# One PSUM bank per tile, weights loaded by ScalarE's queue among the tiles, in a retention and two-layer kernel

## The chip, the core and the metric

The kernel runs on one core of a Trainium2 chip. The metric is the device time of one launch in microseconds (us). Before the change three runs took 886.78, 886.79 and 888.87 us; their median is 886.79 us.

The core has five engines that run their own instruction streams and wait for one another by semaphores: TensorE (PE, matmuls into PSUM; its weight loads are listed as PEld), VectorE (DVE), ScalarE (ACT), GpSimd (POOL) and SyncE (SP). PSUM has 8 banks of 512 fp32 values in each of 128 partitions; a matmul writes into one bank. DMAs are issued from SP's or ScalarE's queue.

## The reference

```python
def _attn_ref(q, k, v):                  # q, k, v: 4 batches, 8 heads, 576 tokens, 64 per head
    scores = scale * np.matmul(q, k.transpose(0, 1, 3, 2))
    gamma = 1.0 - 2.0 ** (-5.0 - np.arange(H, dtype=np.float32))
    Dmat = np.where(rel >= 0, gamma[:, None, None] ** rel[None, :, :], 0.0)   # rel: row less column
    return np.matmul(scores * Dmat[None, :, :, :], v)

x = attn_out.transpose(0, 2, 1, 3).reshape(B * S, H * D)      # 2304 tokens x 512
h = x @ w_in;  r = np.maximum(h, 0.0);  x = (r * r) @ w_out   # first layer, 512 -> 2048 -> 512
h = x @ w_in2; g = h * np.clip(h + 3.0, 0.0, 6.0) / 6.0       # second layer
out = g @ w_out2
```

The weights arrive as 64-bit floats, two 32-bit words to a number. The kernel decodes them to fp32 on ScalarE and VectorE, and splits operands into a high and a low part for TensorE, so that a product of two fp32 matrices is three passes (high by high, high by low, low by high).

## The kernel before, in words

**Tiles.** Retention runs over 20 tiles of a batch's tokens (four full ones of 128 tokens and a last one of 64 for each batch, batches in pairs). In round `ti` of the loop TensorE makes the scores of tile `ti` (`stage_scores`), VectorE multiplies them by the decay (`ret`), and `values(ti - 1)` follows: scores by values (`stage_values`), the state's update (`stage_state`), queries by the state (`stage_queries`), VectorE's copy into `xall`, and ScalarE's copy of the state (`stage_state_copy`), which the queries of the next tile of the same batch, two rounds on, read. `values(ti)` ends by asking for the data of tile `ti + 5`, since there are five places for tiles (`TOKENS`). The first weights are loaded and decoded among the tiles.

**First layer.** The tokens are cut into four passes (`FIRST`: 768, 512, 512 and 512 tokens; called pass 0 to 3 here), each over 16 chunks of the hidden width. One unit is a pass and a chunk: `emit_h` (12 matmuls of 512 columns, 24 in pass 0), `emit_g` (ScalarE: relu, square, high part; VectorE: low part), a split of weights, and `y_steps` of the unit two back (`LAG`), four steps `m` of three matmuls. Chunk 15 is a pass's last: after each of its four steps ScalarE (even `m`) or VectorE (odd `m`) empties the finished bank into `xall`. In pass 0 the tokens above 512 have sums of their own, `ytail`.

**Second layer.** Three passes of 768 tokens (called A, B and C here), each over 8 pairs of chunks. A pair is seven products of six matmuls (`product`, into `hps`), and between the products run the 12 output steps of the pair before (`ywork`, three matmuls each, into six banks `yps`). In a pass's last six steps VectorE (even `m`) or ScalarE (odd `m`) empties each finished bank into a tile `o`, which a DMA stores.

**PSUM.** The eight banks are held as three tiles of two banks (`two_banks`, tags `p0` to `p2`) and two of one bank (`bank`, 6 and 7). Scores and values turn through the three pairs; the `yps` of steps 0 and 1 are two halves of one tile, those of 2 and 3 of the next, and `ytail` is the third. A wait is put between two instructions on two engines where they use the same tile.

**Order.** It is as written (`manual_schedule`); each engine runs its own instructions in that order. DMAs of both queues take turns in eight semaphores, called slots here: a DMA waits before its issue until the one that had its slot before has landed.

Of the kernel before, what the change touches and what calls it, by code (L numbers as in the profile page):

```python
# [9 lines left out]
F32 = mybir.dt.float32  # L10
# [4 lines left out]
ALU = mybir.AluOpType  # L15
# [9 lines left out]
C = 128  # L25
# [10 lines left out]
LAG = 2  # L36
# [31 lines left out]
def retention_moe_moe2(ctx, tc, qk, qk_last, kv, w_in, w_out, w_in2, w_out2, consts, out):  # L68
# [42 lines left out]
    def bank(i, shape, name):  # L111
        return banks.tile(shape, F32, tag=f"b{i}", name=name)

    ring = {"at": 0}

    def two_banks(i, shape, name):
        return banks.tile(shape, F32, tag=f"p{i}", name=name)

    def next_two(shape, name):
        ring["at"] += 1  # L120
        return two_banks(ring["at"] % 3, shape, name)


    staged = {}

    def load_w(l, c, which):
        turn["stage"] += 1
        if turn["stage"] <= 4:
            t = place(f"t{2 + turn['stage']}", [128, DM], mybir.dt.int64, "stage")
        else:  # L130
            t = stagep.tile([128, DM], mybir.dt.int64, tag="stage", name="stage")
        staged[l, c, which] = t
        if which == 0:
            t = t.rearrange("p (k f) -> p k f", k=KD)
            src = (w_in, w_in2)[l][:, c * 128:(c + 1) * 128].rearrange("(k p) f -> p k f", p=128)
            if l == 0:
                nc.sync.dma_start(out=t[:, ::2], in_=src[:, ::2])
                for e in range(2):
                    nc.sync.dma_start(out=t[64 * e:64 * e + 64, 1::2], in_=src[64 - 64 * e:128 - 64 * e, 1::2])
                return  # L140
        else:
            src = (w_out, w_out2)[l][c * 128:(c + 1) * 128, :]
        nc.sync.dma_start(out=t, in_=src)

    w32, first_in = {}, {}

# [51 lines left out]

    def make_decays():

        for e in range(2):
            nc.vector.tensor_tensor(
                out=decay[:, e], in0=mask.unsqueeze(1).to_broadcast([128, HP, C]),
                in1=gv[:, e].unsqueeze(2).to_broadcast([128, HP, C]), op=ALU.mult,
            )
        for e in range(2):
            own = slice(64 * e, 64 * e + 64)
            nc.vector.tensor_tensor(
                out=decay_last[own], in0=mask[own, own].unsqueeze(1).to_broadcast([64, HP, C // 2]),
                in1=gw[own].unsqueeze(2).to_broadcast([64, HP, C // 2]), op=ALU.mult,  # L210
            )
# [8 lines left out]
    def load_kv(ti):  # L220
        b, i, n = tiles[ti]
        kvt = place(TOKENS[ti % len(TOKENS)][1], [128, 2, H, D], F32, "kvt")
        if n == C:
            nc.sync.dma_start(out=kvt, in_=kv[b, C * i:C * i + n])
        else:
            for e in range(2):
                nc.sync.dma_start(out=kvt[64 * e:64 * e + 64, 1], in_=kv[b, C * i:C * i + n, 1])
        data[ti] += (kvt,)

    def load_tile(ti):  # L230
# [17 lines left out]
    def stage_scores(ti):  # L248
        b, i, n = tiles[ti]
        qkt = data[ti][0]  # L250
        r = place(("ret", "t2")[ti % 2], [128, 2, HP, C], F32, "ret")
        pe = next_two([128, 2, HP, C], "aps")
        for a in range(HP):
            for e in range(2):
                nc.tensor.matmul(  # L255
                    out=pe[keys(n, e), e, a, :n],
                    lhsT=qkt[64 * e:64 * e + 64, 0, a, :n],
                    rhs=qkt[64 * e:64 * e + 64, 1, a, :n],
                    start=True, stop=True,
                )  # L260
        if n == C:
            nc.vector.tensor_tensor(out=r, in0=pe, in1=decay, op=ALU.mult)
        for e in range(2 if n < C else 0):
            own = keys(n, e)
            nc.vector.tensor_tensor(
                out=r[own, e, :, :n], in0=pe[own, e, :, :n], in1=decay_last[own], op=ALU.mult
            )
        rets[ti] = r

# [26 lines left out]
    def stage_values(ti):  # L296
        b, i, n = tiles[ti]
        kvt = data[ti][1]
        r = rets.pop(ti)
        p = next_two([128, 2, 4, C], "vps")[:, :, :2]  # L300

        for a in range(HP):
            for e in range(2):
                to = e ^ a % 2
                nc.tensor.matmul(  # L305
                    out=p[64 * to:64 * to + 64, a % 2, a // 2, :n],
                    lhsT=kvt[keys(n, e), 1, 2 * a + e, :], rhs=r[keys(n, e), e, a, :n],
                    start=a < 2, stop=i == 0, skip_group_check=True,
                )
        return p  # L310

    def stage_queries(ti, p):
        b, i, n = tiles[ti]
        qkt = data.pop(ti)[0]
        for a in range(HP if i else 0):
            for e in range(2):
                own, to = slice(64 * e, 64 * e + 64), e ^ a % 2
                nc.tensor.matmul(
                    out=p[64 * to:64 * to + 64, a % 2, a // 2, :n],
                    lhsT=states[b % 2][i % 2][own, a, :], rhs=qkt[own, 1, a, :n],  # L320
                    start=False, stop=True, skip_group_check=True,
                )
        t = b * S + C * i
        by_bank = lambda x: x.rearrange("p (k j) t -> p j k t", j=2)
        nc.vector.tensor_tensor(
            out=by_bank(xall[:, :, t:t + n]), in0=p[:, :, :, :n], in1=by_bank(gq[:, :, :n]), op=ALU.mult
        )


    def parts(pos):  # L330
# [52 lines left out]
    def emit_h(pos, c):  # L383
        w = wins.pop((pos, c))
        hs = []
        for k, (o, n) in enumerate(parts(pos)):
            h = bank(6 + (c % 2 if pos else k), [128, 512], "hps")[:, :n]
            m = 0
            for kk in range(KD):
                for wp, xp in PASSES:  # L390
# [30 lines left out]
    def y_steps(pos, c):  # L421
# [2 lines left out]

        def step(m):
            if c == 0 and m == 0:
                yb[pos] = [t[:, b] for t in [two_banks(i, [128, 2, 512], "yps") for i in range(2)] for b in range(2)]
                if n > 512:
                    tail = two_banks(2, [128, 2, 2, 256], "ytail")
                    yb[pos] += [tail[:, b] for b in range(2)]  # L430
            w, y = wouts[pos, c], yb[pos]
            for k, (o, size) in enumerate(parts(pos)):
                p = y[m] if k == 0 else y[KD + m // 2][:, m % 2]
# [132 lines left out]
    def y_second(j, state):  # L566
# [3 lines left out]
        def work(w, gt, first, last):  # L570
            def step(m):
                if first and m == 0:
                    state["y"] = [
                        t[:, b] for t in [two_banks(i, [128, 2, DM], "yps") for i in range(n // 256)] for b in range(2)
                    ]
                p = state["y"][m]
                for e, (wp, gpart) in enumerate(PASSES):
                    nc.tensor.matmul(  # L578
# [113 lines left out]
    with tc.manual_schedule():  # L692
# [29 lines left out]
        for ti in range(len(tiles)):  # L722
# [2 lines left out]
                scale_keys(ti + 2)  # L725
            if ti:
                values(ti - 1)
            if 2 <= ti < 2 + AHEAD or ti >= len(tiles) - 4:
                load()
            if ti >= 8 and ti % 2 == 0 and halves[0][0] < -1:  # L730
                decoding = decode(*halves.pop(0)[1:])
                decoding.pop(0)()
                decoding.pop(0)()
            elif decoding:
                for f in decoding:
                    f()
                decoding = []
                next_load()
            if ti in (11, 13, 15, 17):
                split_x(0, (ti - 11) // 2)  # L740
            if ti in (14, 16):
                split_in(0, (ti - 14) // 2, nc.gpsimd)
        values(len(tiles) - 1)
        assert halves[0][0] == -1 and len(xs) == KD and not decoding

        units = [(pos, c) for pos in range(len(FIRST)) for c in range(NCH)]
# [153 lines left out]
```

## Time and profile before

| | |
|---|---|
| Runs | 886.78, 886.79, 888.87 us |
| The profiled execution | 885.24 us, of which the span from first to last instruction is 883.4 us |
| TensorE busy | 844.1 us, 96% of the span, in 4962 matmuls |
| VectorE, ScalarE, GpSimd busy | 524.3, 460.7 and 136.1 us |
| DMA | 184.22 MB, mean 209 GB/s |
| Retention, first layer, second layer | 0 to 70 us, 70 to 492 us, 475 to 883 us |
| Matmul of 512 columns, in the second layer's output steps | 396 ns mean of one; 0.23 us from start to start |

The profiled execution is one run, and its time stands 1.55 us below the median of the three. Matmuls are pipelined: one's duration overlaps the next one's, so that three take 0.70 us from the first's start to the start of what follows. Where idle time is named, it is the time the engine's instructions did not cover, and the name behind it is the one whose end released it.

### The profile page before, as it was taken

How to read it: one execution, taken by the hardware profiler on the slowest of the kernel's cores; microseconds unless marked ns; L12 is line 12 of the kernel's file. 1: busy time of each engine (PE TensorE's matmuls, PEld its weight loads, DVE VectorE, ACT ScalarE, POOL GpSimd, SP SyncE). 2: the span in 40 equal slices, each digit the busy share in tenths (PEclk: the TensorE clock that was granted, in tenths of full speed). 3: DMA queues.
4: the chain of work that ended last, by engine and by line, in shares of the span. 5: the costliest groups of instructions: out<-in, count | busy, mean ns of one | idle time of the engine just before them, and what ended most of it. 6: DMA issues, size and time to landing. Idle time of an engine off the chain costs nothing.

```text
span 883.4 us, 13348 instructions
## 1 busy us (share of the span) xinstructions
PE 844.1 (96%) x4962; PEld 726.7 (82%) x4962; DVE 524.3 (59%) x861; ACT 460.7 (52%) x878; POOL 136.1 (15%) x116
## 2 busy tenths in 40 slices
PE   8799999999999899989999899998999998999997
PEld 7688888887888688868888788897798887788885
DVE  5587777784777767775656445546345546344433
ACT  2257777785777667775665333345333345333332
POOL 2141323321433143312220000000000000000000
PEclk9999999999999999999999999999999999999999
DMA  9983656664777677785685454652664652664521
GB/s 364 322 303 100 194 173 187 190 213 147 256 276 276 226 253 264 272 294 181 224 308 193 164 206 155 215 179 94 257 220 155 214 180 88 261 223 155 210 76 72
DMA packets 67650, 184.22 MB, mean 209 GB/s; under 512 B 6656, under 2 KB 23168, under 8 KB 67584
## 3 DMA queue, kind: packets, MB, share of 16 engines
q1 hardware_dynamic: 66864, 182.22, 59.1%
q10 hardware_dynamic: 720, 1.15, 0.4%
q8 instruction: 39, 0.64, 0.3%
q14 instruction: 27, 0.22, 0.1%
HBM read 147.16 MB, written 36.18 MB: 208 GB/s over the span
## 4 chain that ended last, share of the span: by engine, by line
PE 86%; DMA 4%; ACT 4%; DVE 3%; issue 1%; POOL 0%; SPq 0%; ACTq 0%; DVEq 0%
PE yps L578 22%; PE hps L391 21%; PE hps L612 20%; PE yps L435 19%; PE ytail L435 2%; DMA qkt<-in_qk_dram 1%; DMA kvt<-in_kv_dram 1%; DMA stage<-in_w_in_dram 1%; PE vps L305 1%; DVE o L588 1%; PE aps L255 1%; ACT v L623 1%; ACT r L412 1%; ACT r L411 1%; DMA cst<-in_consts_dram 0%
## 5 line engine op out<-in xcount | busy, mean ns | idle before, releaser
L578 PE MATMUL yps<-wo,g 128*128 128x512 f32 x864 | 229.9, 396 | 12.3 <-DVE o L588 12.3
L435 PE MATMUL yps<-g,wo 128*128 128x512 f32 x768 | 198.3, 395 | 12.1 <-ACT xall L448 11.5
L578 PEld LDWEIGHTS yps<-wo,g 128*128 128x128 f32 x864 | 159.9, 189 | 39.4 <-DVE o L588 15.4
L435 PEld LDWEIGHTS yps<-g,wo 128*128 128x128 f32 x768 | 140.0, 189 | 42.7 <-ACT xall L448 14.8
L391 PE MATMUL hps<-xring,win 128*128 128x512 f32 (+1 forms) x720 | 154.7, 363 | 0.3 <-ACT r L411 0.3
L391 PEld LDWEIGHTS hps<-xring,win 128*128 128x128 f32 x720 | 124.1, 190 | 21.9 <-ACT r L411 0.5
L612 PE MATMUL hps<-xlast,win 128*128 128x384 f32 x576 | 117.9, 340 | 0.0
L612 PEld LDWEIGHTS hps<-xlast,win 128*128 128x128 f32 x576 | 104.7, 190 | 8.8
L417 DVE TENSOR_TENSOR g<-r,g 128x512 fp32r<-128x512 f32 x64 | 47.4, 740 | 76.1 <-ACT g L413 75.7
L631 DVE TENSOR_TENSOR u<-hps,u 128x384 f32<-128x384 f32 x48 | 26.8, 558 | 107.7 <-PE hps L612 107.7
L612 PE MATMUL hps<-xop,win 128*128 128x384 f32 x432 | 87.3, 336 | 0.0
L411 ACT ACTIVATE r<-hps 128x512 f32<-128x512 f32 x80 | 44.0, 550 | 82.5 <-PE hps L391 82.5
L612 PEld LDWEIGHTS hps<-xop,win 128*128 128x128 f32 x432 | 77.6, 188 | 6.6
L625 ACT ACTIVATE g<-c 128x384 fp32r<-128x384 f32 x72 | 37.8, 525 | 84.3 <-DVE c L624 84.3
L623 ACT ACTIVATE v<-c,three 128x384 f32<-128x384 f32 x72 | 44.4, 617 | 36.4 <-DVE c L631 35.4
L391 PE MATMUL hps<-xown,win 128*128 128x512 f32 x240 | 60.2, 392 | 0.0
L650 ACT ACTIVATE c<-hps 128x384 f32<-128x384 f32 x24 | 11.8, 492 | 80.3 <-PE hps L612 80.3
L167 DVE TENSOR_SCALAR a<-a 128x512 f32<-128x512 f32 x64 | 38.5, 602 | 24.7 <-ACT a L163 24.7
L391 PEld LDWEIGHTS hps<-xown,win 128*128 128x128 f32 x240 | 45.3, 190 | 9.3
L187 ACT ACTIVATE win<-w 128x512 fp32r<-128x512 f32 x64 | 39.7, 620 | 24.2 <-DVE w L182 24.1
L412 ACT ACTIVATE r<-r 128x512 f32<-128x512 f32 x80 | 47.2, 590 | 2.6
L624 DVE SCALAR_TENSOR_TENSOR c<-v,c 128x384 f32<-128x384 f32 x72 | 40.0, 555 | 13.4 <-ACT v L623 13.4
(76 smaller groups left out, 987.2 us busy)
## 6 DMA issues: line engine op xcount, KB each, us to landing
wo<-kept SPq DMA_DIRECT2D x96, 512.0 KB, 5.0
win<-kept SPq DMA_DIRECT2D x72, 512.0 KB, 3.6
kept<-ready SPq DMA_DIRECT2D x40, 512.0 KB, 3.8
stage<-in_w_out_dram SPq DMA_DIRECT2D x32, 512.0 KB, 4.3
qkt<-in_qk_dram SPq DMA_DIRECT2D x16, 512.0 KB, 8.3
kvt<-in_kv_dram SPq DMA_DIRECT2D x16, 512.0 KB, 8.7
kept<-wo SPq DMA_DIRECT2D x16, 512.0 KB, 5.1
stage<-in_w_in_dram SPq DMA_DIRECT2D x16, 512.0 KB, 4.1
```

What stands on the lines that cost most here:

```text
L167: nc.vector.tensor_scalar(out=a, in0=a, scalar1=LEAST, scalar2=MOST, op0=ALU.max, op1=ALU.min)
L187: nc.scalar.activation(out=hi, in_=src, func=ACTF.Copy)
L391: nc.tensor.matmul(out=h, lhsT=w[:, wp, kk * 128:kk * 128 + 128], rhs=xs[pos, kk][xp][:, o:o + n], start=m == 0, stop=m == 3 * KD - 1,)
L411: nc.scalar.activation(out=r, in_=hs[k], func=ACTF.Relu)
L412: nc.scalar.activation(out=r, in_=r, func=ACTF.Square)
L417: nc.vector.tensor_tensor(out=lo, in0=src, in1=hi.bitcast(F32), op=ALU.subtract)
L435: nc.tensor.matmul(out=p, lhsT=w[:, wp, m * 128:m * 128 + 128], rhs=g[pos, c][k][:, gpart, :size], start=c == 0 and e == 0 and not (k and ...
L578: nc.tensor.matmul(out=p, lhsT=gt[m // 3][:, gpart, m % 3 * 128:][:, :128], rhs=w[:, wp], start=first and e == 0, stop=last and e == 2,)
L612: nc.tensor.matmul(out=to, lhsT=wl[k][:, half, wp, o], rhs=x[:, xp, f], start=first and m == 0, stop=last and m == 5, skip_group_check=True,)
L623: nc.scalar.activation(out=v, in_=c, func=ACTF.Relu, bias=three)
L624: nc.vector.scalar_tensor_tensor(out=c, in0=v, scalar=6.0, in1=c, op0=ALU.min, op1=ALU.mult)
L625: nc.scalar.activation(out=hi, in_=c, func=ACTF.Copy)
```

## The change

1. **PSUM.** Every PSUM tile is one bank. `two_banks` is gone; `next_bank` turns through banks 0 to 5 for scores and values (two tiles each), later through banks 4 to 7 for `hps` from the third unit of pass 1 on. `yps` are banks 0 to 3 (0 to 5 in the second layer), the two tiles of `ytail` banks 4 and 5. VectorE's product of scores and decay, and its copy of the values, become two instructions, one for each bank.
2. **Weights among the tiles.** The first seven loads are issued from ScalarE's queue and not from SP's, at rounds 1, 3 and 5 (before: 2, 3 and 4) and in the last four. Decoding begins at round 6 and not 8.
3. **Last tiles.** The 64 tokens' values are loaded to both halves of the partitions by one DMA and not two.
4. **Decays.** GpSimd makes half of `decay`, and `decay_last` is made after round 1.

```diff
--- before.py
+++ after.py
@@ -111,20 +111,18 @@
     def bank(i, shape, name):
         return banks.tile(shape, F32, tag=f"b{i}", name=name)
 
-    ring = {"at": 0}
-
-    def two_banks(i, shape, name):
-        return banks.tile(shape, F32, tag=f"p{i}", name=name)
-
-    def next_two(shape, name):
+    ring = {"at": 0, "from": 0, "n": 6}
+
+    def next_bank(shape, name):
         ring["at"] += 1
-        return two_banks(ring["at"] % 3, shape, name)
+        return bank(ring["from"] + ring["at"] % ring["n"], shape, name)
 
 
     staged = {}
 
     def load_w(l, c, which):
         turn["stage"] += 1
+        queue = nc.scalar if turn["stage"] <= 7 else nc.sync
         if turn["stage"] <= 4:
             t = place(f"t{2 + turn['stage']}", [128, DM], mybir.dt.int64, "stage")
         else:
@@ -134,13 +132,13 @@
             t = t.rearrange("p (k f) -> p k f", k=KD)
             src = (w_in, w_in2)[l][:, c * 128:(c + 1) * 128].rearrange("(k p) f -> p k f", p=128)
             if l == 0:
-                nc.sync.dma_start(out=t[:, ::2], in_=src[:, ::2])
+                queue.dma_start(out=t[:, ::2], in_=src[:, ::2])
                 for e in range(2):
-                    nc.sync.dma_start(out=t[64 * e:64 * e + 64, 1::2], in_=src[64 - 64 * e:128 - 64 * e, 1::2])
+                    queue.dma_start(out=t[64 * e:64 * e + 64, 1::2], in_=src[64 - 64 * e:128 - 64 * e, 1::2])
                 return
         else:
             src = (w_out, w_out2)[l][c * 128:(c + 1) * 128, :]
-        nc.sync.dma_start(out=t, in_=src)
+        queue.dma_start(out=t, in_=src)
 
     w32, first_in = {}, {}
 
@@ -198,11 +196,13 @@
 
     def make_decays():
 
-        for e in range(2):
-            nc.vector.tensor_tensor(
+        for e, engine in enumerate((nc.vector, nc.gpsimd)):
+            engine.tensor_tensor(
                 out=decay[:, e], in0=mask.unsqueeze(1).to_broadcast([128, HP, C]),
                 in1=gv[:, e].unsqueeze(2).to_broadcast([128, HP, C]), op=ALU.mult,
             )
+
+    def make_last_decay():
         for e in range(2):
             own = slice(64 * e, 64 * e + 64)
             nc.vector.tensor_tensor(
@@ -223,8 +223,8 @@
         if n == C:
             nc.sync.dma_start(out=kvt, in_=kv[b, C * i:C * i + n])
         else:
-            for e in range(2):
-                nc.sync.dma_start(out=kvt[64 * e:64 * e + 64, 1], in_=kv[b, C * i:C * i + n, 1])
+            twice = kv[b, C * i:C * i + n, 1].unsqueeze(0).to_broadcast([2, n, H, D])
+            nc.sync.dma_start(out=kvt[:, 1], in_=twice)
         data[ti] += (kvt,)
 
     def load_tile(ti):
@@ -249,21 +249,19 @@
         b, i, n = tiles[ti]
         qkt = data[ti][0]
         r = place(("ret", "t2")[ti % 2], [128, 2, HP, C], F32, "ret")
-        pe = next_two([128, 2, HP, C], "aps")
+        pe = [next_bank([128, HP, C], "aps") for e in range(2)]
         for a in range(HP):
             for e in range(2):
                 nc.tensor.matmul(
-                    out=pe[keys(n, e), e, a, :n],
+                    out=pe[e][keys(n, e), a, :n],
                     lhsT=qkt[64 * e:64 * e + 64, 0, a, :n],
                     rhs=qkt[64 * e:64 * e + 64, 1, a, :n],
                     start=True, stop=True,
                 )
-        if n == C:
-            nc.vector.tensor_tensor(out=r, in0=pe, in1=decay, op=ALU.mult)
-        for e in range(2 if n < C else 0):
+        for e in range(2):
             own = keys(n, e)
             nc.vector.tensor_tensor(
-                out=r[own, e, :, :n], in0=pe[own, e, :, :n], in1=decay_last[own], op=ALU.mult
+                out=r[own, e, :, :n], in0=pe[e][own, :, :n], in1=decay[:, e] if n == C else decay_last[own], op=ALU.mult
             )
         rets[ti] = r
 
@@ -297,13 +295,13 @@
         b, i, n = tiles[ti]
         kvt = data[ti][1]
         r = rets.pop(ti)
-        p = next_two([128, 2, 4, C], "vps")[:, :, :2]
+        p = [next_bank([128, 4, C], "vps") for j in range(2)]
 
         for a in range(HP):
             for e in range(2):
                 to = e ^ a % 2
                 nc.tensor.matmul(
-                    out=p[64 * to:64 * to + 64, a % 2, a // 2, :n],
+                    out=p[a % 2][64 * to:64 * to + 64, a // 2, :n],
                     lhsT=kvt[keys(n, e), 1, 2 * a + e, :], rhs=r[keys(n, e), e, a, :n],
                     start=a < 2, stop=i == 0, skip_group_check=True,
                 )
@@ -316,15 +314,15 @@
             for e in range(2):
                 own, to = slice(64 * e, 64 * e + 64), e ^ a % 2
                 nc.tensor.matmul(
-                    out=p[64 * to:64 * to + 64, a % 2, a // 2, :n],
+                    out=p[a % 2][64 * to:64 * to + 64, a // 2, :n],
                     lhsT=states[b % 2][i % 2][own, a, :], rhs=qkt[own, 1, a, :n],
                     start=False, stop=True, skip_group_check=True,
                 )
         t = b * S + C * i
-        by_bank = lambda x: x.rearrange("p (k j) t -> p j k t", j=2)
-        nc.vector.tensor_tensor(
-            out=by_bank(xall[:, :, t:t + n]), in0=p[:, :, :, :n], in1=by_bank(gq[:, :, :n]), op=ALU.mult
-        )
+        for j in range(2):
+            nc.vector.tensor_tensor(
+                out=xall[:, j::2, t:t + n], in0=p[j][:, :2, :n], in1=gq[:, j::2, :n], op=ALU.mult
+            )
 
 
     def parts(pos):
@@ -384,7 +382,8 @@
         w = wins.pop((pos, c))
         hs = []
         for k, (o, n) in enumerate(parts(pos)):
-            h = bank(6 + (c % 2 if pos else k), [128, 512], "hps")[:, :n]
+            own = pos == 0 or pos == 1 and c < LAG
+            h = (bank(6 + (c % 2 if pos else k), [128, 512], "hps") if own else next_bank([128, 512], "hps"))[:, :n]
             m = 0
             for kk in range(KD):
                 for wp, xp in PASSES:
@@ -424,10 +423,9 @@
 
         def step(m):
             if c == 0 and m == 0:
-                yb[pos] = [t[:, b] for t in [two_banks(i, [128, 2, 512], "yps") for i in range(2)] for b in range(2)]
+                yb[pos] = [bank(b, [128, 512], "yps") for b in range(KD)]
                 if n > 512:
-                    tail = two_banks(2, [128, 2, 2, 256], "ytail")
-                    yb[pos] += [tail[:, b] for b in range(2)]
+                    yb[pos] += [bank(KD + b, [128, 2, 256], "ytail") for b in range(2)]
             w, y = wouts[pos, c], yb[pos]
             for k, (o, size) in enumerate(parts(pos)):
                 p = y[m] if k == 0 else y[KD + m // 2][:, m % 2]
@@ -570,9 +568,7 @@
         def work(w, gt, first, last):
             def step(m):
                 if first and m == 0:
-                    state["y"] = [
-                        t[:, b] for t in [two_banks(i, [128, 2, DM], "yps") for i in range(n // 256)] for b in range(2)
-                    ]
+                    state["y"] = [bank(b, [128, DM], "yps") for b in range(n // 128)]
                 p = state["y"][m]
                 for e, (wp, gpart) in enumerate(PASSES):
                     nc.tensor.matmul(
@@ -725,9 +721,9 @@
                 scale_keys(ti + 2)
             if ti:
                 values(ti - 1)
-            if 2 <= ti < 2 + AHEAD or ti >= len(tiles) - 4:
+            if ti in (1, 3, 5) or ti >= len(tiles) - 4:
                 load()
-            if ti >= 8 and ti % 2 == 0 and halves[0][0] < -1:
+            if ti >= 6 and ti % 2 == 0 and halves[0][0] < -1:
                 decoding = decode(*halves.pop(0)[1:])
                 decoding.pop(0)()
                 decoding.pop(0)()
@@ -736,11 +732,14 @@
                     f()
                 decoding = []
                 next_load()
+            if ti == 1:
+                make_last_decay()
             if ti in (11, 13, 15, 17):
                 split_x(0, (ti - 11) // 2)
             if ti in (14, 16):
                 split_in(0, (ti - 14) // 2, nc.gpsimd)
         values(len(tiles) - 1)
+        ring.update({"from": 4, "n": 4})
         assert halves[0][0] == -1 and len(xs) == KD and not decoding
 
         units = [(pos, c) for pos in range(len(FIRST)) for c in range(NCH)]
```

On TensorE, the end of pass 0 in the first layer (chunk 15's steps 1 to 3, then the `hps` of the next unit), before. `yps_1209` holds steps 0 and 1, `yps_1210` steps 2 and 3, `ytail_1211` all four tails:

```order
L435 MATMUL yps_1209<-g_2368,wo_2451 128x512 [waits Activation_49]
L435 MATMUL yps_1209<-g_2368,wo_2451 128x512 x2
L435 MATMUL ytail_1211<-gtail_1071,wo_2451 128x256 x3
L435 MATMUL yps_1210<-g_2368,wo_2451 128x512 x3
L435 MATMUL ytail_1211<-gtail_1071,wo_2451 128x256 [waits Activation_49]
L435 MATMUL ytail_1211<-gtail_1071,wo_2451 128x256 x2
L435 MATMUL yps_1210<-g_2368,wo_2451 128x512 [waits Activation_49]
L435 MATMUL yps_1210<-g_2368,wo_2451 128x512 x2
L435 MATMUL ytail_1211<-gtail_1071,wo_2451 128x256 x3
L391 MATMUL hps_2549<-xown_2212,win_2448 128x512 x2
```

The same place now; the four steps have tiles `yps_1281` to `yps_1284`, the tails `ytail_1285` and `ytail_1286`:

```order
L433 MATMUL yps_1282<-g_2443,wo_2526 128x512 x3
L433 MATMUL ytail_1285<-gtail_1143,wo_2526 128x256 x3
L433 MATMUL yps_1283<-g_2443,wo_2526 128x512 x3
L433 MATMUL ytail_1286<-gtail_1143,wo_2526 128x256 x3
L433 MATMUL yps_1284<-g_2443,wo_2526 128x512 x3
L433 MATMUL ytail_1286<-gtail_1143,wo_2526 128x256 x3
L390 MATMUL hps_2624<-xown_2287,win_2523 128x512 [waits Activation_49]
L390 MATMUL hps_2624<-xown_2287,win_2523 128x512
```

The three waits for ScalarE (`Activation`) inside the steps are gone, and the next unit's first matmul into `hps` waits for ScalarE, which it did not before: its bank, 5, is the one that held `ytail_1286`.

On TensorE, the last steps of pass A of the second layer (steps 0 to 5, between the products P5, P4 and P3 and the next pair's P1), before:

```order
L578 MATMUL yps_5029<-wo_5925,g_5782 128x512 x2
L578 MATMUL yps_5029<-wo_5925,g_5782 128x512 [waits DVE_49]
L578 MATMUL yps_5029<-wo_5925,g_5782 128x512 x2
L612 MATMUL hps_5986<-xlast_4880,win_5803 128x384 [waits DMAHW5_49]
L612 MATMUL hps_5986<-xlast_4880,win_5803 128x384 x5
L578 MATMUL yps_5030<-wo_5925,g_5782 128x512 x3
L578 MATMUL yps_5030<-wo_5925,g_5783 128x512 [waits DVE_49]
L578 MATMUL yps_5030<-wo_5925,g_5783 128x512 x2
```

and now:

```order
L574 MATMUL yps_5110<-wo_6009,g_5866 128x512 x2
L574 MATMUL yps_5111<-wo_6009,g_5866 128x512 x3
L608 MATMUL hps_6070<-xlast_4961,win_5887 128x384 [waits DMAHW1_49,DVE_49]
L608 MATMUL hps_6070<-xlast_4961,win_5887 128x384 x5
L574 MATMUL yps_5112<-wo_6009,g_5866 128x512 x3
L574 MATMUL yps_5113<-wo_6009,g_5867 128x512 x3
```

The odd steps wait for VectorE no more; the same holds for step 5 and for the other two passes' ends.

On ScalarE, the first rounds of tiles, before (`sps_172` and `sps_211` are the states of the two batches; each row with `x3` ends a tile's copy):

```order
L291 ACT_TABLE_LOAD [waits DMAHW0_49]
L291 ACTIVATE state_84<-sps_172,cst_81 128x64 [waits PE_49]
L291 ACTIVATE state_84<-sps_172,cst_81 128x64 x3
L291 ACTIVATE state_84<-sps_211,cst_81 128x64 [waits PE_49]
L291 ACTIVATE state_84<-sps_211,cst_81 128x64 x3
```

and now (`sps_175` and `sps_224`):

```order
L289 ACT_TABLE_LOAD [waits DMAHW0_49]
L289 ACTIVATE state_84<-sps_175,cst_81 128x64 [waits PE_49]
L289 ACTIVATE state_84<-sps_175,cst_81 128x64 x3
L135 DMA stage_194<-in_w_in_dram 128x2x128 [waits DMAHW2_49]
L137 DMA stage_194<-in_w_in_dram 64x2x128 [waits DMAHW4_49]
L137 DMA stage_194<-in_w_in_dram 64x2x128 [waits DMAHW5_49]
L289 ACTIVATE state_84<-sps_224,cst_81 128x64 [waits PE_49]
L289 ACTIVATE state_84<-sps_224,cst_81 128x64 x3
```

The three DMAs of a `w_in` load, with their waits for DMA slots (`DMAHW`), now stand in ScalarE's stream between one tile's state copy and the next one's.

## Rows read from the trace of the kernel before

**Rows 1.** waits of TensorE, whole span: engine, line, releaser, us in total, times, longest

```profile
PE yps L578 <- DVE o L588: 12.3, 9, 1.9
PE yps L435 <- ACT xall L448: 11.5, 7, 2.3
```

**Rows 2.** timeline of TensorE, end of pass 1: start, us, instruction, idle before

```profile
299.47 0.84 PE L435 MATMUL yps<-g,wo 128*128 128x512 f32 x3
302.64 1.66 PE L435 MATMUL yps<-g,wo 128*128 128x512 f32 x6 [2.33 <-ACT xall L448]
...
305.79 2.90 PE L391 MATMUL hps<-xring,win 128*128 128x512 f32 x12
```

**Rows 3.** chain of waits, end of pass 2: start us, us, what

```profile
387.57 2.73 PE hps L391 x12
...
402.13 2.74 PE yps L435 x12
```

**Rows 4.** windows, after those waits: us, five engines' busy, granted clock, DMA share, GB/s

```profile
396.00:398.00 2.00, 1.96 (x5) 1.57 (x6) 0.21 (x1) 1.10 (x2) 0.00 (x0) 0.50 0.02 6
```

**Rows 5.** timeline, end of pass 0, TensorE and ScalarE

```profile
205.35 2.90 PE L391 MATMUL hps<-xown,win 128*128 128x512 f32 x12
...
210.64 0.58 ACT L448 ACTIVATE xall<-yps 128x512 f32<-128x512 f32 x1
...
215.13 2.90 PE L391 MATMUL hps<-xown,win 128*128 128x512 f32 x12
```

**Rows 6.** timeline of TensorE, end of pass 3, beside the second layer's first products

```profile
482.48 1.22 PE L612 MATMUL hps<-xlast,win 128*128 128x384 f32 x6
483.54 0.86 PE L435 MATMUL yps<-g,wo 128*128 128x512 f32 x3
484.24 1.23 PE L612 MATMUL hps<-xlast,win 128*128 128x384 f32 x6
...
492.51 1.23 PE L612 MATMUL hps<-xop,win 128*128 128x384 f32 x6
```

**Rows 7.** chain of waits, second layer, the fifth product (P5) of five pairs

```profile
595.18 1.06 PE hps L612 x6
...
633.91 1.06 PE hps L612 x6
...
712.34 1.06 PE hps L612 x6
...
728.03 1.06 PE hps L612 x6
...
766.57 1.06 PE hps L612 x6
```

**Rows 8.** timeline, end of pass C, VectorE's first and ScalarE's last store tile

```profile
872.82 0.69 DVE L588 TENSOR_SCALAR o<-yps 128x512 f32<-128x512 f32 x1 [3.15 <-PE yps L578]
...
879.52 0.60 ACT L590 ACTIVATE o<-yps 128x512 f32<-128x512 f32 x1 [1.85 <-PE yps L578]
```

**Rows 9.** DMA issues, whole span: output stores, KB each, median us to landing

```profile
out_dram<-o SPq DMA_DIRECT2D x15, 256.0 KB, 2.0
```

**Rows 10.** windows among the tiles (columns as rows 4)

```profile
10.00:20.00 10.00, 8.78 (x172) 8.03 (x176) 5.16 (x6) 3.04 (x14) 3.57 (x4) 1.00 1.03 409
30.00:40.00 10.00, 5.86 (x153) 5.13 (x149) 5.55 (x12) 4.08 (x12) 0.73 (x1) 0.97 1.03 312
```

**Rows 11.** groups by line, whole span: VectorE's scores by decay; busy, mean ns, idle

```profile
L262 DVE TENSOR_TENSOR ret<-aps,decay 128x1024 f32<-128x1024 f32 x16 | 19.4, 1220 | 6.9 <-PE aps L255 6.9
```

**Rows 12.** timeline among the tiles: SP's issue of weights, VectorE's copies of values

```profile
14.46 3.07 SPq L139 DMA_DIRECT2D stage<-in_w_in_dram  x2
...
20.36 0.69 DVE L325 TENSOR_TENSOR xall<-vps,cst 128x512 f32<-128x512 f32 x1 [0.89 <-PE vps L318]
...
23.54 0.69 DVE L325 TENSOR_TENSOR xall<-vps,cst 128x512 f32<-128x512 f32 x1 [0.88 <-PE vps L318]
...
61.57 1.31 SPq L139 DMA_DIRECT2D stage<-in_w_in_dram  x2
```

## Prediction

> **What bounds the kernel now.** I read the waits of TensorE first, then the timeline and the chain of waits at the places they name, then the windows of the tile stage. TensorE is nearly always busy, so the question is where it is not. Two waits stand out [rows 1]: 12.3 us of the second layer's output steps on VectorE's store tiles, and 11.5 us of the first layer's on ScalarE's copies into `xall`. They fall only at the ends of passes. There a step is held until its neighbour, in the other bank of the same tile, has been emptied: the end of pass 1 shows step 1 starting 2.33 us late, behind ScalarE's copy of step 0, which lies in another bank [rows 2]. The idle time is not all of the loss: after the waits at the end of pass 2 the granted clock falls to 0.50, the 1.2 GHz level, while TensorE works on [rows 4]. I therefore price each place by its start-to-start time against an undisturbed stretch, which holds both.
>
> **The change part by part.**
>
> *Ends of passes in the first layer.* Twelve matmuls of 512 columns take 2.73 us undisturbed (the first row of rows 3, a unit's `hps`; its output steps have as many).
> - Pass 1: from the last unit's first output step to the next `hps` 305.79 - 299.47 = 6.32 us; less 2.73 that is 3.59 lost [rows 2].
> - Pass 2: from one `hps` to the output steps two blocks further on 402.13 - 387.57 = 14.56; less 3 x 2.73 that is 6.37 lost, the slow clock's share included [rows 3].
> - Pass 0: from `hps` to `hps` 215.13 - 205.35 = 9.78 [rows 5]. An undisturbed unit there is 12 matmuls of `hps` (2.73) and 12 + 12 of outputs, the second 12 with 256 columns (about half of 2.73): some 6.9. Lost: 2.9.
> - Pass 3: from product to product 492.51 - 484.24 = 8.27. Between them lie two products and three steps; a product takes 483.54 - 482.48 = 1.06, a step 484.24 - 483.54 = 0.70, so 4.22 was due and 4.05 are lost [rows 6].
>
> With a tile to each bank the order now shows no wait inside these steps. What is late next? In pass 1 the next pass writes its first step into bank 0 after one more `hps`; TensorE would be there 2.73 us after step 3, and ScalarE's copy of step 0, late as it is, ended by 302.64 [rows 2], against 299.47 + 2.73 + 2.73 = 304.93. So nothing of it comes back. At pass 0 something does. The third unit's `hps` goes to bank 5, which held the last tails, and waits for ScalarE's copy of them. ScalarE starts on the step-0 copy at 210.64, and four copies at 0.58 to 0.6 us with the last not before TensorE ends at 205.35 + 6.9 = 212.3 puts the release at about 213.1; TensorE waits 0.9 us of the 2.9 it was given [rows 5]. Gain of the four places: 2.0 + 3.6 + 6.4 + 4.05 = 16.0 us. Bounds: nothing of it from the 0.9 upward (17), or a copy's length (0.6) kept at each of the other three (14.2).
>
> *Ends of passes in the second layer.* The fifth product comes every 728.03 - 712.34 = 15.69 us. Two pairs across the end of pass A take 633.91 - 595.18 = 38.73, across that of pass B 766.57 - 728.03 = 38.54 [rows 7]: 7.35 and 7.16 lost. The steps' waits for VectorE are gone from the order. Late next is the store: there are three store tiles, so the fourth to sixth step's emptying needs the first three's DMAs landed, 2.0 us each [rows 9]. Steps now come about every 1.2 us (six steps and two products in 6.3). Putting VectorE's and ScalarE's instructions in their order, I estimate that the last emptying ends some 3 us after the last step; the weights for the next pair's second half stand behind that store in SP's queue, and would then be issued some 6 us before they are needed. I take the full 14.5; the lower bound, weights 2 us later than I reckon and both pass ends losing 1.5 us to it, is 11.5.
>
> *The end.* VectorE empties step 0 from 872.82 and ScalarE step 5 from 879.52 [rows 8]: 6.7 us for five steps that need 5 x 0.70 = 3.5 [rows 6]. The last store starts 3.2 us sooner. Six stores then come within 3.5 us instead of 6.7, and may cost one another something; I take 2.9, bounds 2 to 3.2.
>
> *Among the tiles.* Here the DMA engines bound the first half: their share is 1.03 from 10 to 20 us and from 30 to 40 [rows 10], and in the second of these TensorE is busy for only 5.86 of 10 us. The same bytes must land before the tenth tile, on whichever queue, so the weights' place in the queues (a round earlier, and beside SP's stream and not in it) moves which tile waits, not the sum; the decays and the first tile's VectorE work hide behind the same loads. The rate falls from 409 to 312 GB/s between the two stretches, with the same share. The Trainium skill ("DMA: Bandwidth & Descriptors", Issuing engines are not separate DMA queues) says that DMAs from several engines run on the same 16 DMA engines, and that a second issuing engine saves only the time to issue. By that the stage gains nothing but SP's time; were the low rate one queue's doing, 10 us at 312 would take 7.6 at 409 and the stage would gain about 2.4 us for each such stretch. The full share speaks for the rule, and I count nothing.
>
> VectorE pays for the smaller tiles. An instruction on 1024 elements takes 1220 ns [rows 11], one on 512 takes 690 [rows 12]: a fixed part of about 0.16 us, paid twice more in each of 20 rounds, 6.4 us of VectorE's time. Its cover is that a tile's product is needed only a round later (rounds are 23.54 - 20.36 = 3.18 us [rows 12], VectorE's share of them now 2.2), and the third decoding moves two rounds forward out of the stretch where it competed. If that cover fails in the last ten rounds, it costs 3 us; if the moved decoding relieves them, it returns 1.5.
>
> ScalarE pays for the issues. Two of the three DMAs of a `w_in` load held SP for 3.07 us among the early tiles, waiting for slots, and for 1.31 in the last rounds [rows 12]. On ScalarE they stand before the next state copy, which TensorE needs two rounds, 6.4 us, later; so nothing is due early. In the last four rounds ten issues at about 0.65 (half of 1.31), some 6 us, delay the first decoding after the loop by about that, less the idle time that ScalarE had there, and the first layer's first units by 0 to 1.5 us; I take 0.5. The single load of the last tiles' values saves SP an issue of 0.6 us in each of four rounds, and up to 1 us of transfers; I take 1 for it. Sum of the stage: -0.5 us, bounds -4 to +4.
>
> *Sum.* 16.0 + 14.5 + 2.9 + 0.5 = 33.9 us from the profiled execution's 885.24 (a span of 883.4 and 1.84 around it): 851.3. The median of the runs is 1.55 above the profiled one, so I add that: 852.9, rounded to 853.
>
> **The rivals.**
> *ScalarE becomes the bound at the passes' ends.* It does what it did, in the same order, and TensorE arrives sooner: if at each of the six places the next pass's first write meets a bank not yet empty, the wait comes back there, up to the 2.33 us that it was [rows 2], or 2 us at each, 12 in all: 865. For it: ScalarE's copy of step 0 ended 3 us after step 0 began. Against it: there are a whole `hps` block or a product and a step in between.
> *The clock stays low.* The granted 0.50 [rows 4] might belong to the stretch and not to the waits. Pass 2 lost 6.37 where pass 1, with the same order, lost 3.59, so 2.8 us are the clock's; as much again at the ends of passes A and B makes 8.4 not returned, 861. Against it: a stretch with more idle time spread over it, 10 to 20 us, has 1.00, the 2.4 GHz level [rows 10].
> *ScalarE is held by DMA slots* (slower). The place is the rounds with a load. If the slot of a load's DMA is still in flight, ScalarE stands, and behind it the state copies, then TensorE's queries. A hold of H costs H - 6.4 us beyond the two rounds of slack; it eats the 33.4 us gained elsewhere if each of seven loads holds ScalarE for more than 11.2 us, three to four times the 3.07 seen on SP [rows 12]. At 12 us each the time would be 885.24 + 1.55 - 33.4 + 7 x 5.6 = 893.
> *The tiles of one bank don't remove the waits*, because they are the banks' own: 887. The order has no such wait left, and the waited-for step lies in another bank.
>
> **How the numbers follow.** A measurement here can tell a change of about 0.3%, 2.7 us, from none. My forecast (853; its own range 848 to 860) gets 0.78, ScalarE at the passes' ends 0.09, the clock 0.05, a tile stage that gains more than I allow 0.03, ScalarE held 0.03, no effect 0.02. Low end: 17 + 14.7 + 3.2 at the ends, 4 among the tiles: 886.8 - 38.9 = 848. High end: 14.2 + 11.5 + 2.0 and 4 lost among the tiles: 863, which takes in the clock case and leaves out most of the ScalarE case. Faster 0.95, same 0.02, slower 0.03.
>
> **What would show it.** Right: TensorE's two waits of rows 1 are gone or below 2 us together; from the fifth product to the fifth product across passes 31.4 us; pass 2's 14.56 become 8.2; no granted clock below 1.00 after the tiles; a new wait of about 1 us of `hps` for ScalarE at the end of pass 0; the first layer begins between 67 and 74 us. Wrong: waits of the next pass's first steps for ScalarE or VectorE; low clock in stretches without idle time; ScalarE idle behind DMA slots among the tiles, and TensorE's queries late.

## The result, and the profile after

The changed kernel takes 866.46 us (median of 6 runs, 864.64 to 867.75) against 886.78 before: a ratio of 0.9764, interval 0.975 to 0.9778. That is 20.3 us faster, and 13.5 us slower than predicted, above the range of 848 to 863. The profiled execution took 864.64 us with a span of 862.9.

The ends of the passes came out as predicted. First TensorE's waits after the change (columns as [rows 1]): both rows of the two large waits are gone. Of the passes only the predicted wait for the tails' copy is left, 0.7 us. At the top stand waits for loads among the tiles, 10.5 and 4.1 us; in the kernel before (second block) such waits were 3.7 and 3.0.

```profile
PE aps L255 <- DMA qkt<-in_qk_dram: 10.5, 4, 6.5
PE vps L303 <- DMA kvt<-in_kv_dram: 4.1, 2, 3.7
...
PE hps L390 <- ACT xall L442: 0.7, 1, 0.7
```

```profile
PE aps L255 <- DMA qkt<-in_qk_dram: 3.7, 5, 1.1
PE aps L255 <- DMA qkt<-in_qk_last_dram: 3.0, 2, 1.9
```

TensorE's timeline after the change, at the ends of pass 0, 1 and 3 (against [rows 5], [rows 2] and [rows 6]): 7.76 us from `hps` to `hps` in pass 0, 2.72 for the four last steps of pass 1, and 4.19 from product to product in pass 3.

```profile
218.42 2.90 PE L390 MATMUL hps<-xown,win 128*128 128x512 f32 x12
226.18 1.20 PE L390 MATMUL hps<-xown,win 128*128 128x512 f32 x4 [0.69 <-ACT xall L442]
...
310.63 2.88 PE L433 MATMUL yps<-g,wo 128*128 128x512 f32 x12
313.35 2.88 PE L390 MATMUL hps<-xring,win 128*128 128x512 f32 x12
...
485.36 1.22 PE L608 MATMUL hps<-xlast,win 128*128 128x384 f32 x6
486.42 0.86 PE L433 MATMUL yps<-g,wo 128*128 128x512 f32 x3
...
489.55 0.69 PE L608 MATMUL hps<-xop,win 128*128 128x384 f32 x3
```

The chain of waits after the change, at three places: among the tiles, where two loads now take 13.47 and 14.13 us to land, at the end of pass 2 (8.16 us from `hps` to the steps two blocks on, against [rows 3]), and at the fifth products, 31.36 and 31.38 us for two pairs across the ends of passes A and B (against [rows 7]).

```profile
33.19 13.47 DMA qkt<-in_qk_dram
...
66.66 14.13 DMA kvt<-in_kv_dram
80.92 0.46 PE vps L303 x16
...
395.11 2.72 PE hps L390 x12
397.83 2.72 PE yps L433 x12
400.55 2.72 PE hps L390 x12
403.27 0.91 PE yps L433 x4
...
592.44 1.06 PE hps L608 x6
...
623.80 1.06 PE hps L608 x6
...
717.92 1.06 PE hps L608 x6
...
749.30 1.06 PE hps L608 x6
```

At the end of pass C (timeline) the six emptyings start within 3.40 us, against 6.70 in [rows 8].

```profile
855.54 0.69 DVE L584 TENSOR_SCALAR o<-yps 128x512 f32<-128x512 f32 x1 [3.15 <-PE yps L574]
...
858.94 0.60 ACT L586 ACTIVATE o<-yps 128x512 f32<-128x512 f32 x1 [0.76 <-PE yps L574]
```

What went the other way lies before all this. The first layer's first product begins at 81.65 us, in the kernel before at 70.34 (the two timelines, after and before):

```profile
80.92 0.46 PE L303 MATMUL vps<-ret,kvt 64*64 64x64 f32 x16 [3.70 <-DMA kvt<-in_kv_dram]
81.18 0.54 PE L316 MATMUL vps<-qkt,state 64*64 64x64 f32 x16
81.65 10.08 PE L390 MATMUL hps<-xring,win 128*128 128x512 f32 x48
```

```profile
70.34 8.65 PE L391 MATMUL hps<-xring,win 128*128 128x512 f32 x48
```

TensorE waits for the last tile's values, and then its first 48 matmuls take 1.43 us longer than before: the granted clock of that stretch is 0.83, a mean of the 1.2 and the 2.4 GHz levels, after idle time. The windows after the change (columns as [rows 4]) show both, and how little the DMA engines do near the end of the wait: shares of 0.18 and 0.13, at 65 and 50 GB/s.

```profile
78.00:80.00 2.00, 0.00 (x0) 0.00 (x0) 0.53 (x3) 0.00 (x0) 0.00 (x0) 1.00 0.18 65
80.00:82.00 2.00, 1.08 (x33) 0.99 (x34) 0.26 (x2) 0.00 (x0) 0.00 (x0) 0.84 0.13 50
80.00:90.00 10.00, 9.08 (x68) 7.64 (x69) 3.85 (x8) 4.89 (x10) 0.08 (x1) 0.83 0.21 63
```

So the ends gave 33.9 us (the sum is below), the tiles took 11.3 back and the slow first product 1.43. That leaves 21.2 us; the two spans differ by 20.5.

### The profile page after: what moved, and what is told of

Its sections match the earlier page's. It is cut to its first block, busy times and chain, and to the rows that moved or that the text cites. A ratio compares the mean times of both kernels' runs of the same rounds, so it can differ in the third digit from the quotient of the medians.

```text
span 862.9 us, 13373 instructions
## 1 busy us (share of the span) xinstructions
PE 839.4 (97%) x4962; PEld 728.3 (84%) x4962; DVE 526.2 (61%) x896; ACT 459.5 (53%) x878; POOL 138.5 (16%) x117
## 4 chain that ended last, share of the span: by engine, by line
PE 82%; DMA 6%; issue 5%; ACT 3%; POOL 2%; DVE 2%; SPq 0%; ACTq 0%; DVEq 0%; POOLq 0%
PE yps L574 23%; PE hps L608 20%; PE hps L390 18%; PE yps L433 17%; DMA kvt<-in_kv_dram 2%; DMA qkt<-in_qk_dram 2%; DMA stage<-in_w_in_dram 1%; PE ytail L433 1%; POOL win L186 1%; POOL wo L186 1%; PE vps L303 1%; PE aps L255 1%; ACT r L411 0%; DVE ret L263 0%; ACT r L162 0%
## 5 line engine op out<-in xcount | busy, mean ns | idle before, releaser
L574 PE MATMUL yps<-wo,g 128*128 128x512 f32 x864 | 226.3, 394 | 0.0
L433 PE MATMUL yps<-g,wo 128*128 128x512 f32 x768 | 195.7, 392 | 0.6 <-POOL wo L186 0.5
L608 PE MATMUL hps<-xlast,win 128*128 128x384 f32 x576 | 116.1, 336 | 0.0
```

What stands on the lines that cost most here:

```text
L433: nc.tensor.matmul(out=p, lhsT=w[:, wp, m * 128:m * 128 + 128], rhs=g[pos, c][k][:, gpart, :size], start=c == 0 and e == 0 and not (k and ...
L574: nc.tensor.matmul(out=p, lhsT=gt[m // 3][:, gpart, m % 3 * 128:][:, :128], rhs=w[:, wp], start=first and e == 0, stop=last and e == 2,)
L608: nc.tensor.matmul(out=to, lhsT=wl[k][:, half, wp, o], rhs=x[:, xp, f], start=first and m == 0, stop=last and m == 5, skip_group_check=True,)
```

## The experiments

Theory 1: the one load of a half tile's values, whose source names its 64 rows twice, runs on few of the DMA engines and holds the tile stage. Theory 2: the weights on ScalarE's queue hold it. Theory 3: VectorE's smaller instructions do.

**Each part by itself.** e1 puts the two loads back into the changed kernel; e2 gives the kernel before the one load alone, e3 the banks alone, e4 the queue and the rounds alone. The change's fourth part, the decays, was not run alone.

```diff
 e1, in the changed kernel (e2 is the reverse, in the kernel before)
-            twice = kv[b, C * i:C * i + n, 1].unsqueeze(0).to_broadcast([2, n, H, D])
-            nc.sync.dma_start(out=kvt[:, 1], in_=twice)
+            for e in range(2):
+                nc.sync.dma_start(out=kvt[64 * e:64 * e + 64, 1], in_=kv[b, C * i:C * i + n, 1])
 e4, in the kernel before (e3 takes the diff's PSUM parts alone)
+        queue = nc.scalar if turn["stage"] <= 7 else nc.sync
-            if 2 <= ti < 2 + AHEAD or ti >= len(tiles) - 4:
+            if ti in (1, 3, 5) or ti >= len(tiles) - 4:
-            if ti >= 8 and ti % 2 == 0 and halves[0][0] < -1:
+            if ti >= 6 and ti % 2 == 0 and halves[0][0] < -1:
```

> The changed kernel, with the half tiles' values loaded by two DMAs of 64 partitions again, one to each half. Theory 1 (the one load that reads its rows twice moves its 256 KB at a small part of the DMA engines' rate, and held the tile stage about 11 us): the values of the last tile land within 8 us of their issue and not after 14.13; the first matmul of the first layer's hps starts between 70 and 74 us and not at 81.65; time 853 to 859 us. Theory 2 (the weights on ScalarE's queue, their places and the DMA slots held the stage): the first hps stays after 79 us, time 862 us or more. Theory 3 (VectorE's smaller instructions and the tiles of one bank held it): as theory 2 in the time.

> The kernel before, with the one load of the half tiles' values to both halves alone. Theory 1 (that load is slow): 8 to 12 us slower than before, 894 to 899 us, with the window before the first hps at a DMA share near 0.13. Theories 2 and 3: within 2 us of before, 885 to 889 us. The prediction on record counted it as a gain of 1 us.

> The kernel before, with the tiles of one bank alone (and VectorE's instructions split by bank); weights, decoding and values as before. Theory 1: the tile stage ends where it did, first hps between 70 and 73 us, and the ends of the passes give the 33 us of the prediction: 851 to 857 us. Theory 3 (the smaller tiles hold the tile stage): first hps after 77 us, 860 us or more.

> The kernel before, with the weights among the tiles on ScalarE's queue, loaded in rounds 1, 3 and 5, and decoding from round 6, alone. Theory 1: small, 884 to 890 us, first hps between 69 and 74 us (70.34 before). Theory 2: first hps after 77 us, 893 us or more.

Measured, with 887.79 for the kernel before beside them, and the start of the first `hps` in each profile:

| kernel | us | ratio to before (interval) | first `hps` |
|---|---|---|---|
| before | 887.79 | | 70.34 |
| e1, two loads | 855.77 | 0.9644 (0.9623 to 0.9665) | 74.56 |
| e2, one load alone | 898.17 | 1.0118 (1.0096 to 1.014) | 79.77 |
| e3, banks alone | 852.41 | 0.9604 (0.9582 to 0.9626) | 70.06 |
| e4, queue and rounds alone | 889.32 | 1.002 (1.0006 to 1.0033) | 72.43 |

The one load costs 10.7 us in the changed kernel (866.46 against 855.77) and 10.4 alone. The banks alone give 35.4 us, and their tiles end where they did: theory 3 falls, VectorE's smaller instructions are covered. e1's first `hps` came at 74.56 and not before 74, just outside what theory 1 allowed, and e1 is 3.4 us above e3 (the intervals just touch, the single runs don't overlap): something of theory 2 is true as well. In the kernel before, the queue and the rounds together cost 1.5 us (e4). In e2's chain of waits the slow load stands as in the changed kernel, and ahead of it the load of the eleventh tile, a plain one of 512 KB that came behind two of the slow ones:

```profile
29.70 15.97 DMA qkt<-in_qk_dram
...
67.14 11.87 DMA kvt<-in_kv_dram
```

The changed kernel's window from 80 to 82 us does not show the slow load by itself: from 80.2 us on only ScalarE's queue (`q10`) still moved bytes, weights that had been issued after it. In e2 there is a stretch in which only the slow loads of the values moved, from 71 to 72 us, and its share is 0.13 as well, at 49 GB/s (first the changed kernel's DMA view from 80.2 to 82, then e2's window):

```profile
q10 hardware_dynamic: 45, 0.09, 13.1%
...
71.00:72.00 1.00, 1.00 (x24) 1.00 (x24) 1.00 (x1) 0.00 (x0) 1.00 (x1) 1.00 0.13 49
```

**What makes the load slow.** e5 keeps one load of 256 KB to 128 partitions, but from 128 rows in a row; e6 reads two groups of 64 rows that lie apart, none twice.

```diff
-            twice = kv[b, C * i:C * i + n, 1].unsqueeze(0).to_broadcast([2, n, H, D])
 e5
+            twice = kv[b, C * i - n:C * i + n, 1]
 e6
+            twice = kv[b].rearrange("(a t) j h d -> a t j h d", t=n)[2 * i - 4:2 * i + 1:4, :, 1]
```

> The changed kernel, whose one load of a half tile's values reads 128 consecutive rows and not 64 rows twice: the first 64 partitions get the values of 64 earlier tokens, so half of the heads' last outputs are other numbers. As many bytes, the same 128 partitions, still one load. If the slow thing is the source in two groups of 64 rows (theory 1a) or the reading of the same rows twice (theory 1b): as fast as two loads, 853 to 859 us, first hps near 74.6 us, the load landing within 8 us. If it is one load in the place of two (theory 1c): 863 us or more, landing after 13 us or more.

> The changed kernel, whose one load of a half tile's values reads two groups of 64 rows that lie 256 rows apart and no row twice: the first 64 partitions get the values of other tokens, so half of the heads' last outputs are other numbers. Theory 1a (the source's outermost dimension of 2 sets how many DMA engines share the load): as slow as the change, 863 to 869 us, landing near 14 us, a DMA share near 0.13 while it alone is under way. Theory 1b (the same rows read twice): 853 to 859 us.

e5 took 855.11 us (ratio 0.964, interval 0.9615 to 0.9665), as two loads do, and e6 866.49 (0.9764, 0.9743 to 0.9785), as the change. One load in the place of two is not the cost, nor is the double reading; the source in two groups is. In e5 the four loads land after (the line's own view):

```profile
DMA to landing us min/median/max: 2.9/6.1/8.4
```

and in e6 the last one stands in the chain for 14.23 us, while the windows have the share of e2's, with the slow loads alone (33 to 34 us), and of the change's, at the end:

```profile
29.62 16.82 DMA qkt<-in_qk_dram
...
66.56 14.23 DMA kvt<-in_kv_dram
```

```profile
33.00:34.00 1.00, 1.00 (x36) 0.96 (x32) 0.26 (x1) 0.78 (x4) 0.00 (x0) 1.00 0.13 51
80.00:82.00 2.00, 1.07 (x33) 0.99 (x33) 0.00 (x0) 0.00 (x0) 0.00 (x0) 0.50 0.14 52
```

**What ScalarE's queue costs.** e7 is e1 with all weights on SP's queue; e9 adds another bank for the third unit of pass 1; e10 is e9 with the last four weights on ScalarE's queue again. e8 is e3 with that bank and with the first three weights later.

```diff
 e7, in e1 (e10: nc.scalar if 4 <= turn["stage"] <= 7 else nc.sync)
-        queue = nc.scalar if turn["stage"] <= 7 else nc.sync
+        queue = nc.sync
 e8, e9, e10
-        ring.update({"from": 4, "n": 4})
+        ring.update({"at": 1, "from": 4, "n": 4})
 e8, in e3
-            if 2 <= ti < 2 + AHEAD or ti >= len(tiles) - 4:
+            if 4 <= ti < 4 + AHEAD or ti >= len(tiles) - 4:
```

> The changed kernel with two loads for the values and the weights among the tiles on SP's queue again, in rounds 1, 3 and 5 as in the change. Theory 2a (a load on ScalarE's queue takes the DMA slot that SP's next tile load must wait for): the 3.4 us between two loads (855.77) and banks only (852.41) come back, 851 to 854 us, first hps near 70 us. Theory 2b (the rounds and the earlier decoding cost them): 855 to 858 us, first hps near 74.5 us.

> Banks only, with the first three weights loaded two rounds later (rounds 4 to 6) on SP's queue, so that the tiles' loads go first, and with the third unit of pass 1 writing bank 6 and not 5. If TensorE's wait of 0.7 us for ScalarE's tail copy goes and the tiles up to the tenth come 1 to 2 us sooner: 849 to 851 us. If the DMA engines' full share among the tiles only moves the wait to a later tile: 851.5 to 852.5 us.

> Two loads for the values, all weights on SP's queue in rounds 1, 3 and 5, and the third unit of pass 1 writing bank 6 and not 5. If TensorE's 0.7 us wait for ScalarE's tail copy at the end of pass 0 is a real loss: 849.5 to 850.5 us, 0.7 below the 850.7 with bank 5, and the wait of hps on that copy is gone from the trace. If something else ends there as late: 850.5 to 851.5 us.

> As e9, but the last four weights among the tiles on ScalarE's queue, the first three on SP's. Theory 2a (ScalarE's loads harm where SP's tile loads must still come through the shared slots): most of the 5 us between two loads (855.77) and SP's queue (850.7) belongs to the first three, so 850 to 851.5 us, the first hps between 68 and 69.5 us, the sixth tile's load not held for 6 us. If ScalarE's own standing behind its issues is what costs: 852.5 to 855 us, first hps after 71 us.

| kernel | us | ratio to before (interval) | first `hps` |
|---|---|---|---|
| e7, SP's queue | 850.70 | 0.9588 (0.9568 to 0.9607) | 68.06 |
| e8, later weights | 850.87 | 0.9597 (0.9574 to 0.962) | 69.94 |
| e9, SP's queue, other bank | 850.91 | 0.9591 (0.9562 to 0.962) | 70.58 |
| e10, last four on ScalarE | 849.81 | 0.9583 (0.9555 to 0.9612) | 69.33 |

e7 is 5.1 us below e1 (the intervals don't touch) and a little under the range of theory 2a, which it bears out: the rounds are the same, the queue is not. e10 keeps that gain with four of the seven weights on ScalarE's queue, so the first three cost it. In e1, SP's own waits and its timeline show how: the load of the seventh tile stands for 6.8 us until a weight's load of ScalarE's, with which it shares no byte, has landed.

```profile
SPq L217 <- DMA stage<-in_w_in_dram: 6.8, 1, 6.8
```

```profile
14.78 0.33 SPq L224 DMA_DIRECT2D kvt<-in_kv_dram  x1
21.89 0.33 SPq L217 DMA_DIRECT2D qkt<-in_qk_dram  x1
```

In e7's timeline SP issues that load at 14.70, behind the weight itself:

```profile
12.15 1.88 SPq L136 DMA_DIRECT2D stage<-in_w_in_dram  x2
14.70 0.34 SPq L216 DMA_DIRECT2D qkt<-in_qk_dram  x1
```

The wait for the slot is shown; what the two queues' bytes take from one another beside it was not measured apart. Nor is it shown how the wait becomes 5.1 us: among the tiles TensorE waits 6.7 us for loads in e1 and 5.9 in e7, but 4.4 us for VectorE's `ret` in e1 and 1.6 in e7. e9's other bank removes the wait it was meant for (`hps` follows `hps` in 6.92 us at the end of pass 0, 7.76 with bank 5), but its time doesn't differ from e7's. The first `hps` of the two, with one order among the tiles, differ by 2.5 us, so a single profile tells no smaller differences there. e7 to e10 are not to be told apart, nor are e7 and e8 from e3; so nothing is seen here of the decays and the rounds, which e7 has beside the banks. Each of them beats both kernels; e10, the lowest, takes 16.7 us less than the change.

## Why the prediction was right and where it failed

| step | forecast | rows before less rows after |
|---|---|---|
| end of pass 0 | 2.0 | 9.78 - 7.76 = 2.0 |
| end of pass 1 | 3.6 | 6.32 - 2.72 = 3.6 |
| end of pass 2 | 6.4 | 14.56 - 8.16 = 6.4 |
| end of pass 3 | 4.05 | 8.27 - 4.19 = 4.1 |
| ends of passes A and B | 14.5 | 38.73 - 31.36 + 38.54 - 31.38 = 14.5 |
| the end | 2.9 | 6.70 - 3.40 = 3.3 |
| all of it | 33.4 | 33.9; 35.4 in e3's time |
| among the tiles | 0.5 | -11.3, and -1.4 for the clock behind it |

*The ends of the passes.* Every step held, the new wait for the tails among them (0.69 us forecast as 0.9; the end, 3.3, lies 0.1 above its bounds), and neither ScalarE nor the clock became a bound there. (For the stores the forecast took a step as 1.2 us, where its own six steps and two products in 6.3 us make 1.05; TensorE's large wait of [rows 1] in the second layer is gone whole, so nothing hung on it.) Pricing a place by start to start, and not by its idle time, is what made the sizes right: the longest wait anywhere in the first layer was 2.3 us [rows 1], and pass 2 alone gave back 6.4.

*The failed step* is "The single load of the last tiles' values saves SP an issue of 0.6 us in each of four rounds, and up to 1 us of transfers; I take 1 for it." It counted bytes and issues, and not how the load is shared out. Its sign was wrong and its size 10.4 to 10.7 us, beyond the bounds of 4 for the whole stage. Two of the signs named in the forecast failed with it: the first layer began at 81.65 us and not by 74, and the clock stood below 1.00 after the tiles. Before, two loads of 128 KB landed within 7.5 us at most; with the slow loads alone under way, the share is 0.13 (e2 and e6), about two sixteenths. The Trainium skill ("DMA: Bandwidth & Descriptors", Rules for kernel authors) says that a leading repeat of c copies confines a DMA to at most c of the 16 engines. By that the change's load ran on two. The traces of e2 and e6 agree, with 0.13 against 2/16 = 0.125; e6 shows that it is the leading two and not the repeat. The rest of the harm is to others. The plain load of the eleventh tile was issued at 33.19 us, no later than in e1 (33.93), and took 13.47 us; TensorE began that tile's scores at 46.79, in e1 at 39.95. That such a load lands only when two crowded engines have done their part of it is inferred from this; no run tests it alone. The tile puts the change 6.84 us behind e1. By the last tile's scores it is 4.15 behind, since in e1 TensorE waits for VectorE's `ret` for 3.4 us on the way and here for 0.7; the wait of 3.70 us for the last tile's values then makes it 7.1 at the first `hps`. TensorE's timelines, three rows of e1 and one of the change:

```profile
39.95 1.16 PE L255 MATMUL aps<-qkt 64*128 64x128 f32 x16
...
70.71 0.63 PE L255 MATMUL aps<-qkt 64*64 64x64 f32 x16
...
74.56 8.62 PE L390 MATMUL hps<-xring,win 128*128 128x512 f32 x48
```

```profile
74.86 0.63 PE L255 MATMUL aps<-qkt 64*64 64x64 f32 x16
```

*A second step of the same part* failed by less: "The same bytes must land before the tenth tile, on whichever queue, so the weights' place in the queues [...] moves which tile waits, not the sum". It cost 5.1 us (e1 against e7). The rival "ScalarE is held by DMA slots" had the mechanism, but what it cost came with the roles exchanged: SP, held by ScalarE's load, could not afford to stand. ScalarE did stand in the changed kernel, idle for 7.01 us until the last slow load had landed and three weights' loads were issued; TensorE's wait for it after that is 0.3 us, as in the kernel before.

*VectorE's and ScalarE's covers* held. Two instructions of 512 elements take 2 x 0.683 us in e3, against 1.220 in [rows 11], but its first `hps` began at 70.06, and among the tiles TensorE waits for VectorE for 3.1 us, against 2.7 before. For ScalarE, e10 with the last four weights on its queue is no slower than e9 with none. A low rate among the tiles comes with two queues as well: with the weights on ScalarE's queue, 20 to 30 us has a share of 0.95 at 302 GB/s in e1, as slow as the 312 of [rows 10].

## What to carry to other kernels

Fewer and larger loads pay only if the outermost dimension of the source lets all DMA engines share them; here two plain loads beat one that leads with a 2. A load put on an idle engine's queue still takes a place in the slots that the busy queue waits for, so it belongs where nothing urgent follows. The loss at a stalled place is its time from start to start against an undisturbed stretch, since the slow clock after the stall is part of it.

## What the runs showed of the hardware

- Loads whose source leads with a dimension of 2 moved 49 to 51 GB/s at a DMA share of 0.13 while nothing else moved (e2 and e6). The last of them took 11.87 to 14.23 us for 256 KB, in part beside weights; as many bytes from 128 rows in a row landed after 6.1 us (median, e5).
- Loads behind such loads are late too: plain loads of 512 KB issued behind two of them took 13.47, 15.97 and 16.82 us (the change, e2, e6), where before the median of these loads is 8.3 and the longest of their line 11.4.
- The granted clock fell with the idle time that it made: 0.69 from 40 to 50 us and 0.83 from 80 to 90 in the changed kernel, and 0.50, the 1.2 GHz level, from 80 to 82 in e6.
